# A second batch's kv products moved up into the wait for the first Newton iteration, and weight blocks reordered

## The chip, the cores and the metric

The kernel runs on one core of a Trainium2 chip. The metric is device time in microseconds, the median of several executions. The engines are named TensorE (PE), VectorE (DVE), ScalarE (ACT), GpSimd (POOL) and SyncE (SP); SyncE issues nearly all DMAs.

## What is computed

```python
kv = einsum('bhsd,bhse->bhde', k, v)         # batch 8, heads 8, seq 576, dim 64
out = einsum('bhsd,bhde->bhse', q, kv)
x = out / sqrt(mean(out * out, -1) + 1e-06) * g_norm
x = x.transpose(0, 2, 1, 3).reshape(4608, 512)
h = x @ w_in                                 # 512 -> 2048
x = (h * cos(h)) @ w_out                     # 2048 -> 512
a, b = x @ w1, x @ w2                        # 512 -> 1024 each
y = (a * b @ w3) @ w_out2                    # 1024 -> 512
```

## The kernel before, in words

Float32 products are made from two halves: a tile is split into a high part (ScalarE) and the rest, low (VectorE), and `three` issues high x high, high x low and low x high. The weights arrive as 64-bit words; a `Chunk` is a block of 128 x 512 of them. `load` brings it (512 KB), `convert` makes float32 of it in one ScalarE and four VectorE instructions, and `put` splits it into its place (one ScalarE, one VectorE). In the first MLP the block i_m is w_in of the m-th 128 hidden columns, and u_m is w_out of them, m from 0 to 15.

The tokens are taken in 9 blocks t of 512. A step n of the first MLP makes h_n (four times `three`, 12 products of 512 columns), then r, u, sine, u times h, the split into g_n, and later w_n, 12 products of g_n with w_out into four accumulators. The list `steps` first has t = 0 with m = 0 to 7, which are the first eight steps, then t = 1 with m = 0 to 15, then the rest of t = 0, then the others.

Attention works on pairs of heads p = 0 to 3 and on halves of a batch (units u of 288 tokens). For batches 0 and 1 it runs at the very start, written out by hand: `load_first` (L407) gives the loads, `first_batch` (L510) makes kv(0,p), the out products, squares and their sums, then a Newton iteration (`norms`, L492) on VectorE for the inverse root, then for each pair the spread products that copy its result over the partitions, the scaling on VectorE (L507) and the split into x(0). Then `first_steps` (L569) runs the first eight steps with the work of batch 1 between: kv(1,p) in step 0, from step 1 a pair p in each step (out, squares, keeps, sums), norms in step 5, spreads (`rows`) and scalings from step 6, and the conversion of up to two blocks a step, the later half of whose VectorE work falls into the next step. At its end x(1) is split. The order of TensorE, VectorE and ScalarE inside this region is as written (`manual_schedule`); each of them takes its instructions in order. SyncE's and GpSimd's lists are made by the planner of the language, ahead of the run.

Buffers that matter: the main part of kv(1,p) (512 KB) uses the buffer of kv(0,p), q(1,p) (288 KB) that of q(0,p); `kvrest`, the last tokens of all pairs of a batch (256 KB), has one buffer for both batches, and every kv(b,p) ends with four products on it. The words of blocks have eight buffers, so the first eight blocks find theirs fresh, and the ninth (i5) needs the conversion of the first (i0). kv and the second batch's out share two PSUM banks; a kv is copied out by ScalarE (`copy_kv`).

The order of blocks is given by `first_pairs` (L212): i0 i1 i2 u0 i3 u1 i4 u2 i5 u3 i6 u4 i7 u5 i8 u6 i9 u7 and so on. Four are converted in `first_batch`, 13 in the eight steps, and from step 8 one a step (L1155).

Of the kernel before, what the change touches and what calls it, by code (L numbers as in the profile page):

```python
# [13 lines left out]
P = 128  # L14
# [19 lines left out]
def kernel(  # L34
# [177 lines left out]
    def first_pairs():  # L212


        pairs = [(0, 0), (1, 0)]
        for m in range(2, NM):
            pairs += [(m, 0), (m - 2, 1)]
        pairs += [(NM - 2, 1), (NM - 1, 1)]
        free = list(range(NM // 2, NM))
        for m, s in pairs:  # L220
            if s == 1 and m in free:
                free.remove(m)
            tag = f"wo{free[0]}" if free else "bc"
            free = free[1:] + free[:1]
            nm, put = (("i", put_w_in), ("u", put_w_out))[s]
            src = w1pair[m, :, 2 * CHUNK * s:2 * CHUNK * (s + 1)]
            chunks.append(Chunk(f"{nm}{m}", src, tag, put(m)))
# [179 lines left out]
    def load_first():  # L407

        def kv(b, p, q):
            t = wpool.tile(  # L410
                [P, 2, NC, P], F32, tag=f"wi{NM - 2 * NPAIR + p}", name=f"kvraw_{b}_{p}"
            )
            q.dma_start(
                out=t.rearrange("p i c f -> p (i c f)"),
                in_=kv_main[b, p].rearrange("p i c f -> p (i c f)"),
            )
            kv_raw[b, p] = t

        def rest(b, q):
            t = ap.tile([P, NPAIR // 2, 2, P], F32, tag="rest", name=f"kvrest_{b}")  # L420
            q.dma_start(
                out=t.rearrange("p g i f -> p (g i f)"),
                in_=kv_tail[b].rearrange("p g i f -> p (g i f)"),
            )
            kv_rest[b] = t

        def qs(b, p, q):
            t = wpool.tile([P, 2, HALF], F32, tag=f"wi{NM - NPAIR + p}", name=f"q_{b}_{p}")
            q_raw[b, p] = t
            q.dma_start(out=t, in_=qt[b, p].rearrange("u d s -> d u s"))  # L430

        qs(0, 0, nc.scalar)
        qs(0, 1, nc.scalar)
        for h in range(2):
            nc.scalar.dma_start(
                out=gneg[D * h:D * h + D], in_=g_norm.rearrange("(d o) -> d o", o=1)
            )
        kv(0, 0, nc.sync)
        rest(0, nc.sync)
        kv(0, 1, nc.sync)  # L440
        prefetch(1)
        kv(0, 2, nc.sync)
        prefetch(2)
        qs(0, 2, nc.sync)
        prefetch(3)
        kv(0, 3, nc.sync)
        prefetch(4)
        qs(0, 3, nc.sync)
        prefetch(8)
        rest(1, nc.sync)  # L450
        for p in range(NPAIR):
            kv(1, p, nc.sync)
        for p in range(NPAIR):
            qs(1, p, nc.sync)

    whole = []

# [52 lines left out]
    def first_batch(spread, x, y, t):  # L510

        sums = ps_h.tile([P, 512], F32, tag="h", name="ms_first")
        units = range(NHALF)
        count = [1, 1, 1, 1]

        def pieces(n):
            made = [c.convert() for c in chunks[state["conv"]:state["conv"] + n]]
            state["conv"] += n
            for st in made:
                next(st)  # L520
            return made

        def rest_of(made):
            for _ in range(4):
                for st in made:
                    next(st)

        emit_kv(0, 0)
        copy_kv(0)
        made = None  # L530
        for p in range(NPAIR):
            for u in units:
                emit_whole(u, p, ps_acc.tile(
                    [P, 512], F32, tag=f"acc{(2 * p + u) % 4}", name=f"out_{u}_{p}"
                )[:, 0:HALF])
            for u in units:
                emit_square(u, p)
            if p == 0:
                made = pieces(count[0])
            if p < 3:  # L540
                rest_of(made)
            if p > 0:
                put(1)
            if p + 1 < NPAIR:
                emit_kv(0, p + 1)
                copy_kv(p + 1)
            if p == 0:
                nc.scalar.activation(gneg, gneg, AF.Copy, scale=-1.0)
            for u in units:
                emit_sums(u, p, sums, fresh=True)  # L550
            for u in units:
                emit_keep(u, p)
            if p == 2:
                rest_of(pieces(count[3]))
            if p < 2:
                made = pieces(count[p + 1])
        norms(sums, x, y, t)
        put(1)
        for p in range(NPAIR + 1):
            if p < NPAIR:  # L560
                for u in units:
                    ps = ps_acc.tile(
                        [P, 512], F32, tag=f"acc{(2 * p + u) % 4}", name=f"spread_{u}_{p}"
                    )
                    emit_rows(u, p, ps, y, spread)
            if p > 0:
                split_x(0, p - 1)

    def first_steps(spread, x, y, t):  # L569

        units = range(NHALF, 2 * NHALF)
        banks, spread_ps = {}, {}

        def begin():
            st = chunks[state["conv"]].convert()
# [4 lines left out]
        def each():  # L580
            for st in pair:
                next(st)

        def out_bank(v, p):
            if p == 0:
                banks[v] = ps_a.tile([P, 512], F32, tag="pa", name=f"out_{v}")
            emit_whole(v, p, banks[v][:, 0:HALF])

        def rows(p):
            for v in units:  # L590
# [10 lines left out]
        pair = [begin(), begin()]  # L601
        emit_h(0)
        emit_h(1)
        for n in range(HM):
            p = n - 1
            begins = 2 if n < 5 else 1 if n == 5 else 0
            new = []

            if n == 1:
                for v in units:  # L610
                    out_bank(v, 0)
            if n >= 2:
                emit_w(n - 2)
            if n == 6:
                rows(0)
            if 1 <= n < HM - 1:
                emit_h(n + 1)

            if n == 0:
                for _ in range(3):  # L620
                    each()
            r = stage([P, TB], I32, f"r_{n}")
            u = row(f"u_{n}")
            nc.scalar.activation(r, h_ps[n], AF.Identity, bias=0.25, scale=INV_2PI)
            nc.vector.scalar_tensor_tensor(u, h_ps[n], INV_2PI, r, ALU.mult, ALU.subtract)
            if n == 5:
                norms(sums, x, y, t)
            if n == HM - 1:
                scale(1)
                rows(2)  # L630
            if n > 0:
                each()
                each()
            nc.scalar.activation(u, u, AF.Sin, bias=HALF_PI, scale=TWO_PI)
            if n == HM - 1:
                for c in range(2):
                    split_x(1, c)
            if 0 <= p < NPAIR:
                for v in units:
                    emit_square(v, p)  # L640
            if begins > 0:
                new.append(begin())
            nc.vector.tensor_tensor(u, u, h_ps.pop(n), ALU.mult)
            if n > 0:
                each()
            if n == 6:
                scale(0)
                rows(1)
            g_hl[n] = m1.tile([P, 2, TB], F32R, tag="g", bufs=2, name=f"g_{n}")
            since.extend([h_last.pop(n), *split(g_hl[n], u, nc.vector)])  # L650
            if n == 0:
                for k in range(NPAIR):
                    emit_kv(1, k)
                    if k < 2:
                        copy_kv(k)
            if 0 <= p < NPAIR:
                for v in units:
                    emit_keep(v, p)
                sums = banks[units[0]][:, HALF:HALF + NR]
                for v in units:  # L660
                    emit_sums(v, p, sums)
                if p + 1 < NPAIR:
                    for v in units:
                        out_bank(v, p + 1)
            if begins > 1:
                new.append(begin())
            each()
            put(len(pair))
            if n == 0:
                for k in (2, 3):  # L670
                    copy_kv(k)
            pair = new
            prefetch(min(state["put"] + 8, n_first))
        mm = emit_w(HM - 2)
        scale(2)
        rows(3)
        split_x(1, 2)
        scale(3)
        return [mm, *split_x(1, 3)]

    NEWTON, LAST = 8, 10
# [415 lines left out]
    if True:  # L1097
# [49 lines left out]
        for n in range(HM, NS + 2):  # L1147
# [4 lines left out]
            stages = []  # L1152
            if n == NM + HM:
                load["alone"] = False
            ahead = 10 + n  # L1155
            more = min(n_first, ahead) - state["conv"] if n < NS else 0
            if n < NS:
                with tc.issue_after(word_loads[min(n + 9, n_first - 6, len(word_loads) - 1)].ins):
# [234 lines left out]
```

## Time and profile before

| | before |
|---|---|
| median of 3 runs | 1512.69 us (1509.87 to 1514.87) |
| the profiled execution's own time | 1511.92 us |
| its span, first to last instruction | 1509.9 us |
| TensorE busy (matmul) | 1484.7 us, 98% |
| VectorE, ScalarE, GpSimd busy | 868.0, 674.5, 348.8 us |
| mean granted TensorE clock | 0.994 |

The profile is one execution. Times in rows are microseconds from the start of the span. Engines are listed by their short names, PEld is TensorE's loading of stationary tiles, SPq and ACTq are DMA issues. A row of a timeline gives start, duration, engine, line, operation, out<-in, shape and count, and in brackets the idle time before it and what ended it. "busy" on TensorE includes modelled ends, so neighbouring products overlap in the rows; their pace is read from start to start.

### The profile page before, as it was taken

What the parts mean: (1) busy time and instruction counts of PE and PEld (TensorE: products, weight loads), DVE (VectorE), ACT (ScalarE), POOL (GpSimd) and SP (SyncE); (2) the same over time, 40 slices, a digit from 0 to 9 for tenths busy, and PEclk for the clock granted to TensorE, in tenths of its full rate; (3) what the DMA queues carried; (4) which work ended last, traced back from release to release, by engine and by line L of the source; (5) the groups of instructions that cost most, each with busy time, mean ns of one, the idle gap of its engine ahead of it and who ended that gap; (6) DMA issues with size and microseconds to landing.
All of it is one profiled execution on the core that took longest, in us unless ns stands there. A gap on an engine that the chain in (4) does not pass through costs nothing.

```text
span 1509.9 us, 20573 instructions
## 1 busy us (share of the span) xinstructions
PE 1484.7 (98%) x7728; PEld 1268.9 (84%) x7728; DVE 868.0 (57%) x1558; ACT 674.5 (45%) x1356; POOL 348.8 (23%) x278
## 2 busy tenths in 40 slices
PE   7999999999999999999999999999999999999998
PEld 6777888888887887878888887999999998999997
DVE  5988745565555655655655337754554656545543
ACT  5745644544454454544534335533443334433331
POOL 1000010110101101101001007535534327344330
PEclk8999999999999999999999999999999999999999
DMA  9414332334324334343222024122211323223312
GB/s 361 154 63 149 94 104 84 106 100 133 116 86 137 100 103 141 123 125 106 70 87 91 0 76 161 42 84 70 70 45 68 112 71 105 92 84 126 126 63 77
DMA packets 81299, 155.02 MB, mean 103 GB/s; under 512 B 11232, under 2 KB 36944, under 8 KB 81200
## 3 DMA queue, kind: packets, MB, share of 16 engines
q1 hardware_dynamic: 80224, 152.08, 30.8%
q8 instruction: 60, 0.98, 0.3%
q0 software_dynamic: 272, 1.05, 0.2%
q10 hardware_dynamic: 704, 0.59, 0.1%
q14 instruction: 39, 0.32, 0.1%
HBM read 112.57 MB, written 41.12 MB: 102 GB/s over the span
## 4 chain that ended last, share of the span: by engine, by line
PE 90%; DVE 3%; DMA 3%; ACT 1%; issue 1%; POOL 1%; SPq 0%; ACTq 0%; DVEq 0%
PE X L1000 13%; PE x L767 9%; PE h L767 8%; PE x L768 8%; PE x L769 8%; PE h L768 8%; PE h L769 8%; PE V L1000 6%; PE o L768 4%; PE o L767 4%; PE o L769 4%; PE Y L1000 3%; PE kv L277 1%; DMA q<-in_qt_dram 1%; DMA i_w<-in_w1pair_dram 1%
## 5 line engine op out<-in xcount | busy, mean ns | idle before, releaser
L1000 PE MATMUL X<-xc,w 128*128 128x384 f32 x1152 | 224.8, 336 | 4.1 <-DVE wchl L114 1.9
L768 PE MATMUL x<-g,w_out 128*128 128x512 f32 x576 | 225.3, 391 | 0.0
L767 PE MATMUL x<-g,w_out 128*128 128x512 f32 x576 | 222.4, 395 | 2.4 <-ACT w_out L112 2.4
L769 PE MATMUL x<-g,w_out 128*128 128x512 f32 x576 | 223.7, 389 | 0.0
L786 DVE SCALAR_TENSOR_TENSOR u<-h,r 128x512 f32<-128x512 f32 x136 | 94.0, 691 | 210.2 <-ACT r L784 207.6
L767 PE MATMUL h<-x,w_in 128*128 128x512 f32 x544 | 214.6, 395 | 0.0
L768 PE MATMUL h<-x,w_in 128*128 128x512 f32 x544 | 212.8, 391 | 0.0
L1000 PEld LDWEIGHTS X<-xc,w 128*128 128x128 f32 x1152 | 203.0, 188 | 11.6 <-ACT s L1008 3.2
L769 PE MATMUL h<-x,w_in 128*128 128x512 f32 x544 | 212.6, 391 | 0.0
L114 POOL TENSOR_TENSOR xc<-x2r,xc 128x768 fp32r<-128x768 f32 x70 | 134.5, 1930 | 228.7 <-ACT xc L112 228.7
L784 ACT ACTIVATE r<-h 128x512 int32<-128x512 f32 x136 | 81.2, 597 | 205.8 <-PE h L769 196.6
L114 POOL TENSOR_TENSOR qhl<-q,qhl 128x288 fp32r<-128x288 f32 x48 | 40.3, 841 | 454.7 <-ACT qhl L112 454.7
L112 ACT ACTIVATE g<-u 128x512 fp32r<-128x512 f32 x144 | 91.0, 632 | 119.8 <-DVE u L791 84.3
L114 DVE TENSOR_TENSOR g<-u,g 128x512 fp32r<-128x512 f32 x144 | 102.8, 714 | 58.4 <-ACT g L112 58.2
L1008 ACT ACTIVATE s<-X 128x384 f32<-128x384 f32 x144 | 66.7, 488 | 152.5 <-PE X L1000 152.3
L767 PEld LDWEIGHTS x<-g,w_out 128*128 128x128 f32 x576 | 108.2, 188 | 25.9 <-ACT w_out L112 2.8
L769 PEld LDWEIGHTS x<-g,w_out 128*128 128x128 f32 x576 | 108.2, 188 | 22.6
L768 PEld LDWEIGHTS x<-g,w_out 128*128 128x128 f32 x576 | 108.3, 188 | 22.2
L767 PEld LDWEIGHTS h<-x,w_in 128*128 128x128 f32 x544 | 102.5, 188 | 25.3 <-DVE u L791 3.4
L769 PEld LDWEIGHTS h<-x,w_in 128*128 128x128 f32 x544 | 102.5, 188 | 21.3
L791 DVE TENSOR_TENSOR u<-u,h 128x512 f32<-128x512 f32 x136 | 93.0, 684 | 47.4 <-ACT u L790 47.2
L768 PEld LDWEIGHTS h<-x,w_in 128*128 128x128 f32 x544 | 102.5, 188 | 20.2
(177 smaller groups left out, 2477.8 us busy)
## 6 DMA issues: line engine op xcount, KB each, us to landing
x2r<-x_all SPq DMA_DIRECT2D x44, 384.0 KB
kvraw<-in_kv_main_dram SPq DMA_DIRECT2D x32, 512.0 KB
x_all<-x2s SPq DMA_DIRECT2D x36, 256.0 KB
part<-o SPq DMA_DIRECT2D x36, 256.0 KB
part<-part SPq DMA_DIRECT2D x36, 256.0 KB
out_dram<-part SPq DMA_DIRECT2D x36, 256.0 KB
i_w<-in_w1pair_dram SPq DMA_DIRECT2D x16, 512.0 KB
u_w<-in_w1pair_dram SPq DMA_DIRECT2D x16, 512.0 KB
```

The source lines that it names most:

```text
L112: hi = nc.scalar.activation(dst[:, 0], src, AF.Copy)
L114: lo = lo_engine.tensor_tensor(dst[:, 1], src, f32(dst[:, 0]), ALU.subtract)
L277: nc.tensor.matmul(ps[d], k[:, d], v[:, d], start=fresh and i == 0, stop=i == NC, skip_group_check=True,)
L767: nc.tensor.matmul(ps, w[0], x[0], start=first, stop=False)
L768: nc.tensor.matmul(ps, w[0], x[1], start=False, stop=False)
L769: return nc.tensor.matmul(ps, w[1], x[0], start=False, stop=last).ins
L784: nc.scalar.activation(r, h_ps[n], AF.Identity, bias=0.25, scale=INV_2PI)
L786: nc.vector.scalar_tensor_tensor(u, h_ps[n], INV_2PI, r, ALU.mult, ALU.subtract)
L791: nc.vector.tensor_tensor(u, u, h_ps.pop(n), ALU.mult)
L1000: nc.tensor.matmul(ps, w[:, self.i, a, k], x[:, b, k], start=first and k == 0 and n == 0, stop=last and k == 1 and n == 2, skip_group_chec ...
L1008: copied.append(nc.scalar.activation(s, ps, AF.Copy).ins)
```

## The change

Three things are changed. The order of the blocks: the blocks of m = 0 to 7 all come first, so the 15th to 18th are u6, u7, i8, i9 and no longer i8, u6, i9, u7. The second batch: kv(1,0) to kv(1,3) and their copies move from step 0 to `first_batch`, ahead of its norms and of its spreads; its first out products follow the first spreads; its pairs go through steps 0 to 3, its norms come in step 4, its spreads and scalings in steps 5 and 6, and w6 and three quarters of x(1) in step 7. Twelve blocks are begun for the eight steps, and from step 9 on one a step, two in steps 12, 16 and 20. The loads: prefetch(8), which loads the 5th to 8th block (i3, u1, i4, u2), stands behind q(1,1) and no longer ahead of kvrest(1).

```diff
     def first_pairs():
-        pairs = [(0, 0), (1, 0)]
-        for m in range(2, NM):
-            pairs += [(m, 0), (m - 2, 1)]
-        pairs += [(NM - 2, 1), (NM - 1, 1)]
+        pairs = []
+        for half in range(2):
+            ms = range(NM // 2 * half, NM // 2 * (half + 1))
+            pairs += [(m, 0) for m in ms[:2]]
+            for m in ms[2:]:
+                pairs += [(m, 0), (m - 2, 1)]
+            pairs += [(m, 1) for m in ms[-2:]]
...
         qs(0, 3, nc.sync)
-        prefetch(8)
         rest(1, nc.sync)
         for p in range(NPAIR):
             kv(1, p, nc.sync)
         for p in range(NPAIR):
             qs(1, p, nc.sync)
+            if p == 1:
+                prefetch(8)
...
                 made = pieces(count[p + 1])
+        for p in range(NPAIR):
+            emit_kv(1, p)
+            if p < 2:
+                copy_kv(p)
         norms(sums, x, y, t)
         put(1)
+        for p in (2, 3):
+            copy_kv(p)
         for p in range(NPAIR + 1):
             if p < NPAIR:
...
                     emit_rows(u, p, ps, y, spread)
+            if p == 0:
+                for v in range(NHALF, 2 * NHALF):
+                    out_bank(v, 0)
...
+        begins = (2, 2, 2, 1, 2, 1, 0, 0)
         for n in range(HM):
-            p = n - 1
-            begins = 2 if n < 5 else 1 if n == 5 else 0
+            last = n == HM - 1
+            attends = n < NPAIR
             new = []
-
-            if n == 1:
-                for v in units:
-                    out_bank(v, 0)
             if n >= 2:
                 emit_w(n - 2)
-            if n == 6:
-                rows(0)
+            if n in (5, 6):
+                rows(2 * n - 10)
             if 1 <= n < HM - 1:
                 emit_h(n + 1)
-
+            if last:
+                mm = emit_w(n - 1)
...
-            if n == 5:
+            if n == NPAIR:
                 norms(sums, x, y, t)
-            if n == HM - 1:
+            if n == 6:
                 scale(1)
-                rows(2)
             if n > 0:
                 each()
-                each()
+            each()
             nc.scalar.activation(u, u, AF.Sin, bias=HALF_PI, scale=TWO_PI)
-            if n == HM - 1:
-                for c in range(2):
+            if last:
+                for c in range(3):
                     split_x(1, c)
-            if 0 <= p < NPAIR:
+            if attends:
                 for v in units:
-                    emit_square(v, p)
+                    emit_square(v, n)
...
-            if n == 6:
-                scale(0)
-                rows(1)
+            if n in (5, 6):
+                scale(2 * n - 10)
+                rows(2 * n - 9)
+            if last:
+                scale(3)
...
-            if n == 0:
-                for k in range(NPAIR):
-                    emit_kv(1, k)
-                    if k < 2:
-                        copy_kv(k)
...
-        mm = emit_w(HM - 2)
-        scale(2)
-        rows(3)
-        split_x(1, 2)
-        scale(3)
         return [mm, *split_x(1, 3)]
...
-            ahead = 10 + n
+            ahead = 8 + n + (n - 8) // 4
```

## Rows read from the trace of the kernel before

**Rows 1.** Busy time by stretch: PE, PEld, DVE, ACT, POOL, then granted clock, DMA share, GB/s.

```profile
23.00:27.00 4.00, 0.07 (x1) 0.00 (x0) 3.62 (x15) 1.18 (x3) 0.00 (x0) 0.50 1.04 399
27.00:33.00 6.00, 5.87 (x74) 5.90 (x76) 3.44 (x8) 1.86 (x5) 0.00 (x0) 0.50 1.04 393
...
105.00:108.40 3.40, 3.40 (x10) 2.66 (x9) 2.70 (x5) 0.66 (x2) 0.00 (x0) 0.51 0.00 0
108.40:120.00 11.60, 11.60 (x53) 9.47 (x52) 7.22 (x14) 5.47 (x10) 0.00 (x0) 1.00 0.27 92
```

**Rows 2.** Timeline of TensorE, 9 to 46 us.

```profile
9.50 1.12 PE L277 MATMUL kv<-kvraw 128*64 128x64 f32 x16
...
19.22 0.33 PE L277 MATMUL kv<-kvrest 64*64 64x64 f32 x4
...
21.89 1.18 PE L487 MATMUL ms_first<-sel,sq 128*96 128x2 f32 x12
27.14 7.12 PE L500 MATMUL spread<-rs_first 96*64 96x96 f32 x96 [4.07 <-DVE rs_first L370]
...
39.90 0.69 PE L277 MATMUL kv<-kvraw 128*64 128x64 f32 x16
...
44.80 1.24 PE L466 MATMUL out<-q,rs_first 128*128 128x288 f32 x4 [0.90 <-ACT rs_first L462]
```

**Rows 3.** Timeline of SyncE's DMA issues, 15 to 29 us.

```profile
15.57 1.59 SPq L413 DMA_DIRECT2D kvraw<-in_kv_main_dram  x2
...
18.94 0.33 SPq L132 DMA_DIRECT2D i_w<-in_w1pair_dram  x1
20.22 0.38 SPq L430 DMA_DIRECT2D q<-in_qt_dram  x1
22.82 0.33 SPq L413 DMA_DIRECT2D kvraw<-in_kv_main_dram  x1
24.13 0.33 SPq L132 DMA_DIRECT2D u_w<-in_w1pair_dram  x1
25.40 0.38 SPq L430 DMA_DIRECT2D q<-in_qt_dram  x1
26.71 0.33 SPq L413 DMA_DIRECT2D kvraw<-in_kv_main_dram  x1
28.01 0.33 SPq L421 DMA_DIRECT2D kvrest<-in_kv_tail_dram  x1
```

**Rows 4.** Chain of work that ended last, up to 45 us: start, us, what.

```profile
11.25 8.90 DMA i_w<-in_w1pair_dram
...
20.22 10.61 DMA q<-in_qt_dram
```

**Rows 5.** Timeline of VectorE, 34 to 89 us.

```profile
34.97 1.42 DVE L114 TENSOR_TENSOR x<-o,x 128x288 fp32r<-128x288 f32 x4
...
38.96 0.68 DVE L625 SCALAR_TENSOR_TENSOR u<-h,r 128x512 f32<-128x512 f32 x1
...
45.87 0.69 DVE L625 SCALAR_TENSOR_TENSOR u<-h,r 128x512 f32<-128x512 f32 x1 [0.83 <-ACT r L624]
...
52.81 0.68 DVE L625 SCALAR_TENSOR_TENSOR u<-h,r 128x512 f32<-128x512 f32 x1
...
85.64 0.81 DVE L598 TENSOR_TENSOR o<-o,spread 128x288 f32<-128x288 f32 x2
...
88.96 0.68 DVE L625 SCALAR_TENSOR_TENSOR u<-h,r 128x512 f32<-128x512 f32 x1
```

**Rows 6.** Timeline of TensorE, 91 to 111 us: first products of w6, h8, w7 and h11.

```profile
91.41 0.50 PE L767 MATMUL x<-g,w_out 128*128 128x512 f32 x1
...
94.28 0.39 PE L767 MATMUL h<-x,w_in 128*128 128x512 f32 x1
...
103.64 0.50 PE L767 MATMUL x<-g,w_out 128*128 128x512 f32 x1 [2.36 <-ACT w_out L112]
...
110.84 0.39 PE L767 MATMUL h<-x,w_in 128*128 128x512 f32 x1
```

More of the change, by code (lines that the diff above doesn't have):

```diff
@@ L565, in first_batch, with out_bank @@
                     emit_rows(u, p, ps, y, spread)
+            if p == 0:
+                for v in range(NHALF, 2 * NHALF):
+                    out_bank(v, 0)
             if p > 0:
                 split_x(0, p - 1)
+    banks = {}
+    def out_bank(v, p):
+        if p == 0:
+            banks[v] = ps_a.tile([P, 512], F32, tag="pa", name=f"out_{v}")
+        emit_whole(v, p, banks[v][:, 0:HALF])
     def first_steps(spread, x, y, t):
         units = range(NHALF, 2 * NHALF)
-        banks, spread_ps = {}, {}
+        spread_ps = {}
         def begin():
@@ L582, in each @@
                 next(st)
[L584 to L587, printed above, removed]
         def rows(p):
@@ L625, in first_steps @@
             nc.vector.scalar_tensor_tensor(u, h_ps[n], INV_2PI, r, ALU.mult, ALU.subtract)
-            if n == 5:
+            if n == NPAIR:
                 norms(sums, x, y, t)
-            if n == HM - 1:
+            if n == 6:
                 scale(1)
-                rows(2)
             if n > 0:
                 each()
-                each()
+            each()
             nc.scalar.activation(u, u, AF.Sin, bias=HALF_PI, scale=TWO_PI)
-            if n == HM - 1:
-                for c in range(2):
+            if last:
+                for c in range(3):
                     split_x(1, c)
-            if 0 <= p < NPAIR:
+            if attends:
                 for v in units:
-                    emit_square(v, p)
-            if begins > 0:
+                    emit_square(v, n)
+            if begins[n] > 0:
                 new.append(begin())
@@ L645, in first_steps @@
                 each()
-            if n == 6:
-                scale(0)
-                rows(1)
+            if n in (5, 6):
[3 more added lines that the diff above has]
+                scale(3)
             g_hl[n] = m1.tile([P, 2, TB], F32R, tag="g", bufs=2, name=f"g_{n}")
             since.extend([h_last.pop(n), *split(g_hl[n], u, nc.vector)])
-            if n == 0:
-                for k in range(NPAIR):
-                    emit_kv(1, k)
-                    if k < 2:
-                        copy_kv(k)
-            if 0 <= p < NPAIR:
+            if attends:
                 for v in units:
-                    emit_keep(v, p)
+                    emit_keep(v, n)
                 sums = banks[units[0]][:, HALF:HALF + NR]
                 for v in units:
-                    emit_sums(v, p, sums)
-                if p + 1 < NPAIR:
+                    emit_sums(v, n, sums)
+                if n + 1 < NPAIR:
                     for v in units:
-                        out_bank(v, p + 1)
-            if begins > 1:
+                        out_bank(v, n + 1)
+            if begins[n] > 1:
                 new.append(begin())
-            each()
+            if n > 0:
+                each()
             put(len(pair))
-            if n == 0:
-                for k in (2, 3):
-                    copy_kv(k)
             pair = new
             prefetch(min(state["put"] + 8, n_first))
-        mm = emit_w(HM - 2)
-        scale(2)
-        rows(3)
-        split_x(1, 2)
-        scale(3)
         return [mm, *split_x(1, 3)]
```

## The prediction

> **What bounds it now.** I read the page first, then the stretches of the first 120 us, then SyncE's issues, TensorE's and VectorE's timelines there, and the chain of waits. TensorE is busy 98% of the span, so only the places where it stands or is slowed can be won. In the stretches [rows 1] there are two. Between 23 and 27 us it does next to nothing (0.07 of 4.00 us), and from 27 to 33 it is granted 0.50 of its clock; from 105.0 to 108.4 it is granted 0.51, after an idle time of 2.36 us [rows 6]. From 23 to 33 us the DMA engines are full at 393 to 399 GB/s. The first hole is the Newton iteration: the last sums begin at 21.89 and the first spread product starts at 27.14 [rows 2]. The second batch's kv stands later, from 39.90, and its first pair at 44.80 [rows 2]. The change puts those 80 products into the hole. They can only run there if their data has landed, so the loads come first.
>
> **When the loads land.** SyncE issues loads in a list fixed beforehand. A load goes out as soon as the eighth before it has landed: i3, issued at 11.25, landed 8.90 later at 20.15, and q(1,1) went at 20.22; that one took 10.61 and landed at 30.83 [rows 3, 4]. The list behind i3 is [rows 3], with the names that the program gives: u1, i4, u2, kv(1,0) and kv(1,1) at 15.57, q(1,0), i5 at 18.94, q(1,1), kv(1,2), u3, q(1,2), kv(1,3) at 26.71, and the tail block kvrest(1) last, at 28.01. Behind q(1,1) that is 512+512+288+512+256 KB = 2.13 MB, and at 393 to 399 GB/s [rows 1] 5.4 us: the tail lands at 30.83 + 5.4 = **36.2 us**. Before, nobody minded, since kv began at 39.90. Every kv(1,p) ends on its share of that tail, and TensorE takes its products in program order.
>
> The change moves prefetch(8), the blocks i3, u1, i4 and u2 (2.10 MB), behind q(1,1) in the program. Does it bring the tail forward? The list is not program order. i5 is written after q(1,3) and goes out before q(1,1) and kv(1,2); u3 goes before kv(1,3); the tail, written before kv(1,0), goes after kv(1,3) [rows 3]. Whoever plans it takes the first load in program order whose buffer is free by its own clock. kv(1,p) uses the buffer of kv(0,p), and the tail that of the first tail, which TensorE reads last at 19.22 [rows 2]. i3, u1, i4 and u2 have fresh buffers and are free at any time. So in the new list kv(1,0), q(1,0) and kv(1,1) may move up among the four blocks, but kv(1,2), kv(1,3) and the tail can't: their buffers come free late, and until then the four blocks fill the places, and i5 and u3 after them as before. The same bytes stand ahead of the tail. I take 36.2 us.
>
> DMA bandwidth is a point where page and trace differ. The Trainium skill (DMA: Bandwidth & Descriptors, Specifications) gives a core about 358 GB/s of HBM; this trace shows 393 to 399, and by the page's figure the tail would land 0.5 us later and the sum would be 0.5 us higher.
>
> **The sum, part by part.**
> 1. *kv(1) ahead of the spread.* TensorE does the main part of kv(1,0) at 23.1 and then waits for the tail until 36.2. What it does next it does at the lower clock, as the spread did for 6 us after an idle time of 4 us [rows 1]. Sixteen kv products took 1.12 us early on (9.50) and 0.69 at full clock (39.90) [rows 2], so twenty take 1.4 or 0.86. A tail and three whole kv are 0.3 + 3 x 1.4 = 4.5 us (at full clock 2.8). The spread then starts at 40.7 (39.0) and not at 27.14: **13.6 us later** (11.9). The Newton iteration has long ended and hides nothing of it. Queued behind the wait: copy_kv(0) on ScalarE, behind that the split of u0, and on VectorE all that follows Newton. None had anything else to do.
> 2. *Spread to the last part of x(0).* Before, from 27.14 to 34.97 + 1.42 = 36.39 [rows 2, 5], 9.25 us, 6 of them at half clock. New in it are two out products, 1.24 us [rows 2]. The clock should be back some 6 us after 36.2, so most of the slow stretch is already spent on kv; at full clock it would give back at most 3 us. So 7.5 to 10.5 us; I take 8.7, gain 0.5. x(0) is complete **13 us later** (11 to 15).
> 3. *The eight steps.* VectorE sets the pace with 6.94 us for a step with two blocks (45.87 to 52.81), of which three instructions of 0.68, as its u, are the step's own, so a block costs 2.45 us. u_0 to u_7 took 88.96 - 38.96 = 50.0 us [rows 5]. After the change step 0 (6.91 us, to 45.87) has no copies of kv on ScalarE, but the squares and keeps of the first pair; I take 0.3 off, between 0 and 0.6. Up to u_7 VectorE converts 12 blocks and not 13: -2.45. The scalings of pairs 1 and 2 now come ahead of u_7, each 0.81 as the pair at 85.64: +1.6. Gain **1.2 us** (0.5 to 2).
> 4. *From u_7 to the end of h10.* Before 110.84 - 88.96 = 21.9 us. After, TensorE has w5, w6, h8, h9, w7 and h10 left, each 94.28 - 91.41 = 2.87 us [rows 6], 17.2 in all; the spreads of rows(2) and rows(3) are done before. u7 is converted in step 6 and no longer at step 8, so the wait of 2.36 us of w7 for w_out [rows 6] goes, and with it the slow 3.4 us (1.7 lost). What is late next is x(1) for h8; its first three quarters are split in step 7 under w5 and w6. Gain **4.7 us** (3 to 5.5).
> 5. *At no cost.* After step 8 sixteen blocks are left for 13 steps where fifteen had 15. TensorE is busy 11.60 of 11.60 us there and VectorE 7.22 [rows 1], which covers 16 x 2.5; if the three steps with two blocks were not covered, up to 2.5 us each. i8 and i9 are needed only eight steps later. POOL's list keeps its two saves of x(0), 13 us later, with their reader far off.
>
> Sum: +13 - 1.2 - 4.7 = +7.1, so **+7 us** (bounds +3.5 to +11). The profiled execution took 1511.92 us (span 1509.9 and 2.0 around it), 0.8 below the median of 1512.69. So 1518.9 by it, 1519.7 as a median. 0.3%, about what a measurement of this kernel can tell, is 4.5 us.
>
> **The rivals.**
> *A, the loads do come sooner* (the other side). If the four blocks really go behind the tail, it lands 2.10 MB / 396 GB/s = 5.3 us sooner, at 30.9, and the sum is +1.7: 1514.4. It decides at five blocks behind the tail, where +7 is used up; with i5 and u3 behind too (7.9 us) it is -0.9. For it: the move is written for that. Against: rows 3, where program order yields to free buffers. 0.08.
> *B, as the title says.* kv is done by the end of Newton near 27 us: no delay, the clock is kept, the gains of parts 3 and 4 remain: -7, 1505.7. All but the first four blocks would have to stand behind the tail, and its buffer is read until 19.5. 0.05.
> *C, the tail overtakes.* It lands at its issue at 28.01 at the earliest; then kv(1,3), landing one tail (0.7 us) before 36.2, holds the end: spread at 35.5 + 1.4 = 36.9, 3.8 us sooner than in part 1, +3.2, 1515.9. Rows 4 speak against it, as each place comes free in the order of the list. The Trainium skill (the same page, Queues, rings and completion order) says that completion is not first in, first out within an issuing engine; by that rule this case could come, and the trace so far doesn't bear it out. 0.04.
> *D, the delay comes and the gains don't.* VectorE is the pace of the steps, ScalarE is late in step 0, where squares and keeps of the pair now come a step sooner, and the rows wait for scalings on VectorE: +13, 1525.7. 0.08.
>
> **Numbers.** The forecast has 0.75, its own range is 1516.2 to 1523.7. For eight in ten I take in A and C: 1513.5 to 1523.5; B, the rest of A, and most of D stay out. Faster by over 4.5 us is B and a little of A: 0.06. Within 4.5 us: A, C and the lower edge of the forecast: 0.19. Slower: the rest of the forecast and D: 0.75.
>
> **What would show it.** Right: TensorE idle some 12 us before 36 us with kvrest as its releaser; in SyncE's list i5 and u3 still ahead of kv(1,3), and kvrest behind it; spread near 41; first u near 52; granted clock about 0.5 from 36 to 40 or a little more; no wait of w7 for w_out; h10 ending near 118. Wrong: a kvrest that lands before 30, a spread before 32, or no gap closed at w7.

## The result, and the profile after

| | before | after |
|---|---|---|
| median | 1512.69 us (1509.53 to 1518.56, 7 runs) | 1521.32 us (1520.79 to 1523.18, 7 runs) |
| ratio to before, 95% interval | | 1.0056 (1.0037 to 1.0075) |
| the profiled execution, its span | 1511.92, 1509.9 | 1523.18, 1521.1 |

The kernel is slower by 8.6 us by the medians. The spans of the two profiled executions differ by 11.2: after's is the longest of its seven runs, 1.9 above their median, and before's lies 0.8 below its own.

The load issues of SyncE after the change, from 19 to 28 us, which answer to [rows 3] (i5, q(1,1), kv(1,2), u3, q(1,2), kv(1,3) and the tail):

```profile
19.25 0.88 SPq L132 DMA_DIRECT2D i_w<-in_w1pair_dram  x1
21.19 0.38 SPq L433 DMA_DIRECT2D q<-in_qt_dram  x1
21.99 0.33 SPq L416 DMA_DIRECT2D kvraw<-in_kv_main_dram  x1
23.29 0.33 SPq L132 DMA_DIRECT2D u_w<-in_w1pair_dram  x1
24.56 0.38 SPq L433 DMA_DIRECT2D q<-in_qt_dram  x1
25.84 0.33 SPq L416 DMA_DIRECT2D kvraw<-in_kv_main_dram  x1
27.11 0.33 SPq L424 DMA_DIRECT2D kvrest<-in_kv_tail_dram  x1
```

The list ends as it did before: i5 and u3 still go ahead of kv(1,3), and the tail is last. The chain of work that ended last, up to 45 us (start, us, what), shows what this does:

```profile
27.11 8.68 DMA kvrest<-in_kv_tail_dram
35.84 4.86 PE kv L280 x64
40.69 2.12 PE spread L504 x24
42.81 2.22 PE out L470 x4
```

The tail lands at 27.11 + 8.68 = 35.79 us, and from there TensorE makes the rest of kv, and only then the first spread. TensorE's timeline in the same stretch and at h10:

```profile
22.13 1.12 PE L280 MATMUL kv<-kvraw 128*64 128x64 f32 x16
35.84 0.48 PE L280 MATMUL kv<-kvrest 64*64 64x64 f32 x4 [12.58 <-DMA kvrest<-in_kv_tail_dram]
...
40.62 2.19 PE L504 MATMUL spread<-rs_first 96*64 96x96 f32 x24
42.74 2.29 PE L470 MATMUL out<-q,rs_first 128*128 128x288 f32 x4
...
118.39 0.50 PE L769 MATMUL h<-x,w_in 128*128 128x512 f32 x1 [2.08 <-DVE u L793]
```

In [rows 2] the spread began at 27.14; now it is 40.62. The gap of w7 in [rows 6] is gone, and a new one of 2.08 us stands ahead of h10. Busy time by stretch (PE, PEld, DVE, ACT, POOL, granted clock, DMA share, GB/s), to be held against [rows 1]:

```profile
23.00:36.00 13.00, 0.42 (x9) 0.23 (x6) 2.36 (x12) 0.00 (x0) 0.00 (x0) 0.50 1.04 399
36.00:40.00 4.00, 4.00 (x60) 3.41 (x60) 0.69 (x1) 1.94 (x7) 0.00 (x0) 0.50 0.30 116
40.00:43.50 3.50, 3.50 (x36) 2.90 (x33) 0.91 (x2) 1.03 (x4) 0.00 (x0) 0.50 0.01 2
43.50:45.00 1.50, 1.50 (x6) 0.60 (x4) 0.00 (x0) 0.23 (x1) 0.00 (x0) 0.50 0.00 0
45.20:50.00 4.80, 4.80 (x79) 4.05 (x76) 4.19 (x12) 2.40 (x7) 0.53 (x1) 1.00 0.00 0
105.00:108.40 3.40, 3.40 (x16) 2.82 (x16) 3.37 (x12) 2.14 (x8) 0.00 (x0) 1.00 0.36 127
108.40:120.00 11.60, 9.52 (x42) 7.54 (x42) 5.44 (x12) 4.16 (x9) 0.00 (x0) 1.00 0.08 29
```

The clock is 0.50 (1.2 GHz) until about 45.1 us, 9.3 us beyond the end of the wait, and 1.00 (2.4 GHz) from there; the slow stretch at 105 us is gone. VectorE, to be held against [rows 5]: a word block that stood behind the wait, the last part of x(0), and the first u.

```profile
38.95 0.69 DVE L114 TENSOR_TENSOR w_out<-u_f,w_out 128x512 fp32r<-128x512 f32 x1 [13.25 <-ACT w_out L112]
...
49.44 1.43 DVE L114 TENSOR_TENSOR x<-o,x 128x288 fp32r<-128x288 f32 x4
...
53.42 0.68 DVE L638 SCALAR_TENSOR_TENSOR u<-h,r 128x512 f32<-128x512 f32 x1
```

To see where time is won and lost in every kernel below, one set of marks serves: the start of VectorE's u in steps 0, 7 and 30 (step 30 stands at 231.83 us before and at 241.35 after, and from there on the steps keep one distance). All columns in us, one profiled execution each; the medians and ratios are those of the timed runs, each against the kernel before on the same chip.

| kernel | median | ratio (95%) | u_0 | u_0 to u_7 | u_7 to u_30 | u_30 to end |
|---|---|---|---|---|---|---|
| before | 1512.69 | | 38.96 | 50.0 | 142.9 | 1278.1 |
| after | 1521.32 | 1.0056 (1.0037 to 1.0075) | 53.42 | 49.3 | 138.6 | 1279.8 |
| kv in step 0 | 1513.15 | 1.0004 (0.9995 to 1.0013) | 42.28 | 54.5 | 138.6 | 1278.1 |
| fresh buffers | 1512.23 | 0.9993 (0.9982 to 1.0005) | 42.87 | 49.3 | 138.6 | 1277.5 |
| prefetch back | 1522.01 | 1.0058 (1.0045 to 1.0071) | 52.41 | 49.3 | 140.2 | 1278.5 |
| order alone | 1511.97 | 0.9995 (0.9982 to 1.0007) | 42.68 | 50.0 | 143.0 | 1279.6 |
| order alone, again | 1511.30 (one) | | 39.27 | 50.0 | 143.0 | 1277.1 |
| order, w7 behind h9 | 1511.19 | 0.9987 (0.9977 to 0.9998) | 42.52 | 50.0 | 139.3 | 1277.8 |
| tail alone fresh | 1518.67 | 1.0040 (1.0026 to 1.0055) | 49.69 | 49.3 | 140.2 | 1277.4 |
| fresh, out behind h0 | 1509.81 | 0.9979 (0.9968 to 0.9990) | 39.91 | 49.3 | 138.6 | 1279.8 |
| the same, w7 behind h9 | 1509.91 | 0.9981 (0.9971 to 0.9991) | 40.42 | 49.3 | 137.7 | 1278.6 |

After against before: 14.46 lost to u_0, 0.7 won in the eight steps, 4.2 won up to step 30: 9.5 in all. The last column differs by up to 2.7 between these executions (by 2.5 between the two with the order alone), so its 1.7 can't be put down to the change. Nor does all of the 4.2 belong to it: experiments 2 and 3 have the order of after behind u_7 and the same wait of 2.08 ahead of h10, and keep 2.7, since there the clock fell behind that wait and in after's profile it did not (last section).

### The profile page after: what moved, and what is told of

Same layout as the page of the kernel before. It is cut to its first block, busy times and chain, and to the rows that moved or that the text cites. A ratio compares the mean times of both kernels' runs of the same rounds, so it can differ in the third digit from the quotient of the medians.

```text
span 1521.1 us, 20566 instructions
## 1 busy us (share of the span) xinstructions
PE 1484.1 (98%) x7728; PEld 1268.5 (83%) x7728; DVE 867.2 (57%) x1558; ACT 672.6 (44%) x1356; POOL 349.6 (23%) x278
## 4 chain that ended last, share of the span: by engine, by line
PE 90%; DVE 4%; DMA 3%; issue 1%; POOL 1%; ACT 1%; SPq 0%; ACTq 0%; DVEq 0%
PE X L1002 13%; PE x L769 9%; PE h L769 8%; PE x L770 8%; PE x L771 8%; PE h L770 8%; PE h L771 8%; PE V L1002 6%; PE o L770 4%; PE o L769 4%; PE o L771 4%; PE Y L1002 3%; PE kv L280 2%; DMA i_w<-in_w1pair_dram 1%; DMA kvrest<-in_kv_tail_dram 1%
## 5 line engine op out<-in xcount | busy, mean ns | idle before, releaser
L770 PEld LDWEIGHTS x<-g,w_out 128*128 128x128 f32 x576 | 108.2, 188 | 21.9
```

Source lines behind the costliest of these rows:

```text
L770: nc.tensor.matmul(ps, w[0], x[1], start=False, stop=False)
```

## The experiments

**1. Fresh buffers: is it the place of the loads, or that of the products?** TensorE's order stays that of after.

```diff
-    [P, 2, NC, P], F32, tag=f"wi{NM - 2 * NPAIR + p}", name=f"kvraw_{b}_{p}"
+    [P, 2, NC, P], F32, tag=f"wi{NM - (2 + b) * NPAIR + p}", name=f"kvraw_{b}_{p}"
...
-    t = ap.tile([P, NPAIR // 2, 2, P], F32, tag="rest", name=f"kvrest_{b}")
+    if b == 0:
+        t = ap.tile([P, NPAIR // 2, 2, P], F32, tag="rest", name=f"kvrest_{b}")
+    else:
+        t = wpool.tile([P, NPAIR // 2, 2, P], F32, tag="wi3", name=f"kvrest_{b}")
```

> The changed kernel, its kv products in the same place ahead of the spread, but the second batch's kv blocks and tail get fresh buffers and not those of the first batch. Theory (the buffers, not the program order, fix the order of the loads): SyncE issues kvrest and the four kv blocks ahead of q(1,0), i3, u1, i4 and u2, the 2.3 MB of them land by about 27 us, TensorE has done kv by the end of the Newton iteration, the spread starts at 27 to 29 and x(0) is complete near 37: 14 us sooner than in the changed kernel, so 1505 to 1509 us, about 1507. i5, u3 and what follows land later by the same bytes, which nobody waits for. Rival 1 (the blocks pushed back are now late: i3 and u1 hold the first steps): the spread at 27 to 29, but u_0 or u_1 waits for words, 1510 to 1516. Rival 2 (the place on TensorE costs by itself, by the low clock): 1518 to 1522.

Measured: 1512.23 us, 9.1 below after. SyncE's issues and TensorE's products:

```profile
10.84 0.47 SPq L427 DMA_DIRECT2D kvrest<-in_kv_tail_dram  x1
12.41 3.70 SPq L416 DMA_DIRECT2D kvraw<-in_kv_main_dram  x4
17.13 0.38 SPq L436 DMA_DIRECT2D q<-in_qt_dram  x1
```

```profile
24.27 1.12 PE L280 MATMUL kv<-kvraw 128*64 128x64 f32 x16
...
29.71 0.48 PE L280 MATMUL kv<-kvrest 64*64 64x64 f32 x4
30.12 2.19 PE L507 MATMUL spread<-rs_first 96*64 96x96 f32 x24
32.24 2.29 PE L473 MATMUL out<-q,rs_first 128*128 128x288 f32 x4
```

With their own buffers the tail and all four kv blocks are issued ahead of q(1,0) and i3, as the program writes them, and kv runs straight behind the sums without a wait. So the buffers fix the order of the loads, and the wait for them is most of what after loses. The time is 5 us above the 1507 expected: at the low clock the 80 products take 5.85 us, and the spread starts at 30.12, where the Newton iteration alone (4.07 us in [rows 2], behind sums that end at 24.34 here) would have let it start at 28.4. The out pair in the spread lasts 2.2 us more. These two, 3.9 us, eat most of the 5.0 won behind u_0. That they make up the whole 3.9 by which u_0 is later than in the profile of before is partly chance: the sums also end 1.3 us later here, and the spread's own products take 1.8 us less. The time lies in the range of rival 1, but nothing waited for words: TensorE's one long wait in the steps is 2.6 us for ScalarE, ahead of the sums of the second batch's first pair.

**2. The prefetch alone put back.**

```diff
         qs(0, 3, nc.sync)
+        prefetch(8)
         rest(1, nc.sync)
...
             qs(1, p, nc.sync)
-            if p == 1:
-                prefetch(8)
```

> The changed kernel with the request for blocks 5 to 8 (i3, u1, i4, u2) put back ahead of the second batch's loads, and nothing else. Theory (this move brings the tail block no sooner, since the same bytes stand ahead of it either way): kvrest lands at 35.5 to 36.5, as in the changed kernel, the spread starts at 40 to 41.5, and the time is that of the changed kernel within 2 us, 1519 to 1523. Rival (the move did bring the loads forward): the tail block some 5 us later, near 41, and 1525 to 1528 us.

Measured: 1522.01 us. TensorE's timeline:

```profile
25.66 1.12 PE L280 MATMUL kv<-kvraw 128*64 128x64 f32 x16 [2.36 <-DMA kvraw<-in_kv_main_dram]
35.22 0.48 PE L280 MATMUL kv<-kvrest 64*64 64x64 f32 x4 [8.44 <-DMA kvrest<-in_kv_tail_dram]
```

The move of the four blocks brings kv(1,0) forward, 22.13 in after and 25.66 here, and the tail not at all: 35.22 here. No gain of the move shows, as expected.

**3. A fresh buffer for the tail alone.** Only the second edit of experiment 1.

> The changed kernel, with a fresh buffer for the second batch's tail block alone; kv(1,2) and kv(1,3) still use the buffers of the first batch. Theory (it is the order of the loads, and the last of those that kv needs ends the wait): the tail lands near 20, TensorE does kv(1,0) to kv(1,2) as they land, and waits for kv(1,3), which now lands near 35.8; then one kv of 1.4 us and the spread near 37.2, 3.4 us sooner than in the changed kernel: 1517 to 1519. Rival (only the tail is late, and with it early the whole delay of 14 us goes): 1507 to 1513.

Measured: 1518.67 us. TensorE's timeline:

```profile
24.91 0.33 PE L280 MATMUL kv<-kvrest 64*64 64x64 f32 x4
32.42 1.12 PE L280 MATMUL kv<-kvraw 128*64 128x64 f32 x16 [7.18 <-DMA kvraw<-in_kv_main_dram]
...
35.80 1.12 PE L280 MATMUL kv<-kvraw 128*64 128x64 f32 x16 [1.85 <-DMA kvraw<-in_kv_main_dram]
...
37.26 2.19 PE L507 MATMUL spread<-rs_first 96*64 96x96 f32 x24
```

Two kv are done by 25.2, and then kv(1,2) and kv(1,3) hold TensorE. The last load that is needed lands at the same 35.8, whichever it is, since the same bytes stand ahead of it; only the products behind it get fewer.

**4. kv back in step 0, the rest of the change kept.**

```diff
-        for p in range(NPAIR):
-            emit_kv(1, p)
-            if p < 2:
-                copy_kv(p)
         norms(sums, x, y, t)
         put(1)
-        for p in (2, 3):
-            copy_kv(p)
...
-            if p == 0:
-                for v in range(NHALF, 2 * NHALF):
-                    out_bank(v, 0)
...
             nc.scalar.activation(u, u, AF.Sin, bias=HALF_PI, scale=TWO_PI)
+            if n == 0:
+                for p in range(NPAIR):
+                    emit_kv(1, p)
+                    copy_kv(p)
+                for v in units:
+                    out_bank(v, 0)
```

> Everything of the change stays, but the second batch's kv, its copies and the first pair of out go back behind h0 and h1, into step 0. Theory (the whole loss is TensorE standing in line for kvrest): the tail block still lands near 36, nobody waits for it, the spread starts near 27 and x(0) is complete near 36.4, as before the change; u_0 at 39 to 40. The gains of the steps (0.7) and of the stretch behind u_7 (3.3), measured in the changed kernel, stay: 1512.7 - 4.0 = 1508.7 us, 1507 to 1511. Rival 1 (the re-ordered steps and the sixteen blocks for thirteen steps cost, not the wait): 1517 us or more, with idle time behind 120 us. Rival 2 (the gain behind u_7 was only there because the steps started late): within 2 us of the kernel before, 1511 to 1514.

Measured: 1513.15 us, in the range of rival 2, but none of the three has the reason: the wait is gone and the stretch behind u_7 keeps its gain (138.6), but the eight steps take 54.5 us and not 49.3. VectorE in step 0:

```profile
42.28 0.68 DVE L629 SCALAR_TENSOR_TENSOR u<-h,r 128x512 f32<-128x512 f32 x1
...
49.67 0.69 DVE L114 TENSOR_TENSOR g<-u,g 128x512 fp32r<-128x512 f32 x1 [4.92 <-ACT g L112]
...
52.73 0.68 DVE L629 SCALAR_TENSOR_TENSOR u<-h,r 128x512 f32<-128x512 f32 x1
```

All four copies of kv (before, two of them) and the squares now stand on ScalarE ahead of the split of g, and VectorE waits 4.92 us for it; step 0 takes 10.45 us (6.91 before, 6.24 after). So in this arrangement pairs a step sooner need kv made before step 0, and what the change wins in the steps and what it loses ahead of them are not independent. Whether other places for the copies would do was not tried.

**5. The order of the blocks alone,** in the kernel before (the first part of the change's diff), profiled twice.

> The kernel before with the new order of the weight blocks alone. Theory (the gap of 2.36 us ahead of w7 was its w_out, made late because u7 stood behind i8 and i9, and the low clock behind the gap cost 1.7 us): w7 no longer waits for w_out, the clock stays at 1.00 from 100 to 112 us, and the time is 1512.7 - 4.1 = 1508.6, 1507.5 to 1510.5. Rival 1 (another thing is late there, x(1) or the scale of the last pairs, and the gap moves to it): no change, 1511.5 to 1514. Rival 2 (a block that is now converted later holds a step of the main loop): 1512 to 1516 with a wait for w_in there.

> The kernel before with the new block order alone once more, for a second profile of it: the first was that of its slowest execution (1517.3 us, its median 1512.0). Theory (the wait of h10 for h8's last step is the order's own, in every execution): 2 to 3 us idle ahead of h10 again, no wait of w7 for w_out. Rival (it belonged to that execution): h10 waits under 1 us, and the time from the first r to 200 us is some 2.5 us shorter than the 161.9 us of the first profile.

Measured: 1511.97 us, and 1511.30 in the one run of the second profile. u_7 to u_30 is 143.0 in both, as in the kernel before. TensorE's waits from 90 to 125 us in the second profile (in all, times, longest; the first has the same row):

```profile
PE h L770 <- DVE u L794: 3.0, 1, 3.0
```

w7 no longer waits for w_out. But its products then stand among those of h8 and h9, h8 ends later, and h10, whose bank h8's last step on VectorE sets free, waits 2.98 and 2.99 us, each time with the clock down to 0.50 behind it for some 3 us. The gap has moved, and nothing is won: rival 1 in kind.

**6. The order, with w7 held behind h9.**

```diff
-                emit_w(n - 2)
+                with ExitStack() as gate:
+                    if n == HM + 1:
+                        gate.enter_context(tc.issue_after(h_last[n]))
+                    emit_w(n - 2)
```

> The kernel before with the new block order (as in the run with the order alone, 1512.0 us) and w7's products held behind the last of h9's. In the run with the order alone the gap ahead of w7 was gone, but w7's products stood among those of h8 and h9, h8 ended later, and h10, which takes the bank that h8's last step on VectorE sets free, waited 2.98 us. Theory (the gain of the order is there and is lost again to h8's late end): with ten products of w7 (0.23 us each, 2.3 us) no longer ahead of h8's end, the wait of h10 falls below 1 us and the time to 1509 to 1510.5. Rival (VectorE, with two steps and a block in one stretch, sets the time of h10, whatever TensorE's order): the wait stays near 3 us or moves to w8, 1511.5 to 1513.

Measured: 1511.19 us; u_7 to u_30 falls to 139.3, 3.6 less than in the kernel before. The same view:

```profile
PE h L770 <- DVE u L794: 0.7, 2, 0.4
```

So the cause of h10's wait is the place of w7's products. In the timed runs the median, between the two ranges that were given, falls by 1.1 us, with an interval from 0.3 to 3.5 us that overlaps with that of the order alone; how much of the 3.6 a typical run keeps stays open.

**7. Fresh buffers, and the out pair behind h0.**

```diff
-            if p == 0:
-                for v in range(NHALF, 2 * NHALF):
-                    out_bank(v, 0)
...
         emit_h(0)
+        for v in units:
+            out_bank(v, 0)
         emit_h(1)
```

> The run with fresh buffers for the second batch's loads (1512.2 us), with the second batch's first out pair taken out of the spread and put behind h0. That run gained 5.0 us between the first r and 200 us, as the changed kernel did, but its first r came 3.9 us later than in the profile of before: of that 1.8 us are kv, which at the lower clock lasts 5.85 us and ends at 30.19, and 2.2 us the out pair within the spread. Theory (the out pair is on the path to x(0) and to u_0, and off it behind h0): x(0) 1.2 to 2.2 us sooner, 1510 to 1511. Rival (the first step then waits for the squares and sums of that pair, as it has 2.6 us of idle time there already): no change, 1511.5 to 1513.

Measured: 1509.81 us, by the medians 2.4 less than with fresh buffers alone. The ratios to before, 0.9979 and 0.9993, have intervals that overlap, so how much the move of the pair is worth stays open. TensorE's timeline:

```profile
28.08 7.44 PE L507 MATMUL spread<-rs_first 96*64 96x96 f32 x96
35.45 0.50 PE L771 MATMUL h<-x,w_in 128*128 128x512 f32 x1
...
38.30 1.13 PE L473 MATMUL out<-q,rs_first 128*128 128x288 f32 x4
```

Of the 2.96 us by which u_0 comes sooner in this profile, 2.04 are there before the spread starts (28.08 and not 30.12), where the two kernels do the same work; from the spread's start to u_0 it takes 11.83 us and not 12.75. The eight steps take 49.3 as before the move, so the rival's wait costs nothing.

**8. The same, with w7 held behind h9.** Both edits together.

> The run with fresh buffers and the out pair behind h0, and w7's products held behind h9's as well. Theory (each takes away a wait of its own): the wait of h10, 1.18 us with fresh buffers and 2.08 us in the changed kernel, goes, and the time is 1 us below that of the run with the out pair behind h0 alone: 1508.5 to 1510.5, below both kernels. Rival (w8 or x2s is late next): no difference to the run without the hold.

Measured: 1509.91 us. h10's wait falls from 1.2 to 0.3 us and u_7 to u_30 by 0.9, and the median doesn't follow: no difference, as the rival had it, though h10's wait did go. Experiment 7 is the kernel to keep: faster than before by 0.2% (interval 0.1% to 0.3%) and, by the medians, than after by 11.5 us.

## Why the prediction was right

The forecast was slower, at 1519.7 us in a range of 1513.5 to 1523.5; it is 1521.32.

- **The loads** came as argued. The tail was put at 36.2 and landed at 35.79, behind i5, u3 and kv(1,3). Experiments 1 to 3 show the reason that was given: a load whose buffer is still in use goes behind those whose buffers are free, whatever the program says. Rival A, which believed the move of the four blocks, is refuted by experiment 2, and rival C by the tail's place at the end. The Trainium skill (DMA: Bandwidth & Descriptors, Queues, rings and completion order) says that completion need not be first in, first out; no run here shows a load that overtook another.
- **Part 1** put the spread at 40.7; it starts at 40.62, after 12.58 us of idle time. The lower clock, which the sum took from that wait, was there ahead of it: the sixteen kv products at 22.13 already take 1.12 us.
- **Part 2** put x(0) 13 us later (11 to 15); it is complete at 49.44 + 1.43 = 50.87, 14.5 later. The term that was too small is the low clock: taken as 6 us beyond the wait, it lasted 9.3, and so the first 24 spread products and the out pair behind them ran at half pace too; the pair took 2.29 us and not 1.24.
- **Part 3** gave the eight steps 1.2 (0.5 to 2); they won 0.7, within the range but not by its terms. All of it is step 0, which fell from 6.91 to 6.24 us (0.3 was given, at most 0.6). From u_1 to u_7 it takes 43.05 us where it took 43.09, so the 0.85 for a block less and two scalings more did not show: VectorE is busy 0.84 us less there, as the terms have it (40.70 and 41.54), but idle 0.80 more (2.35 and 1.55), which the sum put at nothing.
- **Part 4** gave 4.7 up to the end of h10 (3 to 5.5). The wait of w7 and the slow stretch went, as said. But from u_7 (102.71) to the end of h10 (121.29) it takes 18.6 us where it took 21.9, a gain of 3.3: the sum took TensorE to be without gaps there, and overlooked that h10 needs the bank which h8's last VectorE step frees, 2.08 us. That the loss is no more than 1.4 comes from the six groups of products, which took 2.75 us each and not 2.87. Up to step 30 the gain is 4.2, and 2.7 in the profiles of experiments 2 and 3.
- **Part 5** holds: between step 8 and step 30 nothing is lost to blocks, and TensorE is busy without a gap from 120 to 800 us.

Of the marks that it named, all are there but the last: the first u at 53.42 (near 52 was said), and h10 ends at 121.3 and not near 118. The sum was +7.1 (its upper bound, by its own terms, is +11.5 and not +11) and the mark at step 30 shows +9.5: 1.5 of the difference is part 2, 0.5 part 3, 0.5 part 4. The medians differ by 8.6, between the two; the profiled execution of before has an early u_0 (38.96; 39.27, 42.52 and 42.68 in three profiles with the same instructions up to there), which may make the loss up to u_0 look larger than it is in the middle of the runs; that was not tried. The interval of the ratio, 0.37% to 0.75%, is 5.6 to 11.3 us, so the runs can't tell 7.1 from 9.5, and that the sum comes within 1.5 us of the median is in part luck.

## What to carry to other kernels

Before work is moved into a hole, look when its data lands, and find that in the list of loads as it goes out, not in the program: a load into a buffer that is still read goes behind every load into a free one. When such a move is wanted, give the loads buffers of their own first, and put into the hole only what fits at the clock that rules there. A gap that is closed has a next one behind it: list who waits for the work that is moved, and check which bank or buffer it holds.

## What had not been expected of the hardware

**The front differs from execution to execution.** Four out products of one pair of heads, of one shape each time, from TensorE's timelines of the kernel before and, in the second fence, of the first profile of the order alone, whose instructions are the same up to there:

```profile
12.90 2.27 PE L466 MATMUL out<-q,rs_first 128*128 128x288 f32 x4
17.46 1.22 PE L466 MATMUL out<-q,rs_first 128*128 128x288 f32 x4
```

```profile
18.76 2.27 PE L469 MATMUL out<-q,rs_first 128*128 128x288 f32 x4
24.36 2.27 PE L469 MATMUL out<-q,rs_first 128*128 128x288 f32 x4
```

The products run at half pace at first, until some point before 17.46 in one and beyond 24.36 in the other, although the profile's column grants 1.00 in both. In the second (stretch, busy, granted clock, DMA share, GB/s):

```profile
22.00:26.00 4.00, 4.00 (x22) 1.00 1.03 404
```

So in the front the pace of products of one shape tells the clock, and the column does not. With it u_0 moves by 3.4 us between the two profiles of the order alone (42.68 and 39.27). In the kernels that wait for a load at 35 us the wait would take such a difference up, and their spread is small: 2.4 us over 7 runs of after and 2.2 over 5 of experiment 2, against 9.7 over 29 runs of before. But experiment 3, which waits as well, has 4.6 over 7, and experiment 8, which waits for no load there, 3.5 over 12. That the spread comes from this was not tried. The Trainium skill (TensorE: Matmul & The Clock Gate, Part 1: The HAM clock gate) says that the low one of the two levels is the state in which TensorE starts and that activity lifts it; the products agree with it and the column doesn't.

**The clock can fall while TensorE is busy, and the same wait brings the low clock in one execution and not in the next.** Stretches of TensorE (busy, granted clock, DMA share, GB/s) with fresh buffers:

```profile
14.00:18.00 4.00, 3.29 (x34) 0.92 1.03 403
18.00:24.00 6.00, 6.00 (x33) 0.50 1.03 401
24.00:30.00 6.00, 6.00 (x83) 0.50 1.03 405
```

The clock falls to 0.50 (1.2 GHz) between 17.3 and 17.4 us. The last idle time ahead of that is 0.72 us and ended at 14.71, and the clock stays down through the twelve microseconds from 18 to 30, in which TensorE is busy.

The other half is the wait of h10: its first product and the stretch from 119 to 122 us (all engines, as in the table of stretches above), in experiment 2 and then in after, whose first product, behind the same 2.08 us, is shown at 118.39:

```profile
117.37 0.50 PE L768 MATMUL h<-x,w_in 128*128 128x512 f32 x1 [2.08 <-DVE u L792]
119.00:122.00 3.00, 3.00 (x8) 2.30 (x7) 2.89 (x6) 2.11 (x4) 0.00 (x0) 0.50 0.40 148
```

```profile
119.00:122.00 3.00, 3.00 (x15) 2.45 (x14) 3.00 (x6) 1.30 (x4) 0.00 (x0) 1.00 0.32 120
```

The products are the same, in the same order. The twelve of h10 take 4.25 us in experiment 2, where the clock is at 0.50 (1.2 GHz), and 2.90 in after, where it stays at 1.00 (2.4 GHz); here pace and column agree. Experiment 3 does as experiment 2, and this is the 1.6 us between 140.2 and 138.6 in the table. What decides between the two, these runs don't show.
